# Reading tail keys and values in place, with one mask per step, instead of copying them per step

## The chip, the cores and the metric

The kernel runs on one core of one Trainium2 chip. The metric is the device time of one execution in microseconds, lower is better. The five compute engines appear in the profile as PE (TensorE matmuls), PEld (TensorE weight loads, which overlap PE), DVE (VectorE), ACT (ScalarE) and POOL (GpSimd); SP issues the DMAs.

## The reference, cut to what matters

Four layers run in turn, A B A B, each on a layer norm of a residual stream of 2048 tokens of width 640. Layer A is a segmented linear-memory attention and is not touched, except that its first instance now builds the masks. Layer B is recurrent:

```python
mem = mem0                                   # 8 memory tokens
for s in range(64):                          # segments of 32 tokens
    xs = x[:, 32 * s:32 * s + 32, :]
    h = concatenate([mem, xs])               # 40 tokens
    q, k, v = h @ Wq, h @ Wk, h @ Wv         # 32 heads of 128
    scores = where(mask, q @ k.T * scale, -1e9)   # key j seen by query i if i < 8 or i >= j
    o = (softmax(scores) @ v) @ Wo
    mem = o[:8]                              # the next step waits for this
    outs.append(o[8:])
```

A step can't start before the step before it has produced `mem`. There are 64 steps in a layer, two layers: 128 steps.

## The kernel before: the parts that matter

The 40 tokens of a step are kept as 24 tokens of the segment, 8 memory tokens and the segment's last 8 tokens, the "tail". Queries, keys and values of the tails of four steps (a group, `T`; `i4` is the step's place in it) are projected together, 32 tokens at once, into `QTt`, `KTt` and `Vtb`. Ahead of each step its 8 tails were copied out:

```python
def tails_to_seg(s):
    T, i = divmod(s, 4)
    nc.gpsimd.tensor_copy(heads(QT[s])[:, :, 32:40], QTt[T][:, :, 8 * i:8 * i + 8])
    nc.gpsimd.tensor_copy(heads(KT[s])[:, :, 32:40], KTt[T][:, :, 8 * i:8 * i + 8])
    Vt[s] = qkp.tile([128, 2, 512], BF16, name="b_Vt", tag="Vt")
    for j in range(4):
        nc.sync.dma_start(Vt[s][32 * j:32 * j + 8, :, :], Vtb[T][32 * j + 8 * i:32 * j + 8 * i + 8, :, :])
```

The values went by DMA since a token of `Vtb` is a partition, and the matmuls below read each head's values from the start of a block of 32 partitions. The scores are computed transposed (keys on partitions), four heads side by side in the four column tiles of the array; part `k = 0` has the 32 keys of segment and memory, part `k = 1` the 8 of the tail:

```python
for j in range(4):       # puts the mask into PSUM
    nc.tensor.matmul(sp[32 * j:32 * j + 32, :, 0:40], lhsT=C.identb[:, 32 * j:32 * j + 32], rhs=mask..., ...)
for r in range(4):
    for k, n in ((0, 32), (1, 8)):
        for j in range(4):
            o = sp[32 * j:32 * j + n, r, 16:56] if k == 0 else sp[32 * j:32 * j + n, r, 0:16]
            nc.tensor.matmul(o, lhsT=KT[s][:, 40 * h + 32 * k:40 * h + 32 * k + n],
                             rhs=QT[s][:, 40 * h + 24 * k:40 * h + 40], ...)
# ... exp on ACT into PT, sums with blk, normalise ...
for r in range(4):       # values
    for k, n in ((0, 32), (1, 8)):
        V_ = Vsb if k == 0 else Vt[s]
        for j in range(4):
            nc.tensor.matmul(o, lhsT=V_[32 * j:32 * j + n, b, 128 * r:128 * r + 128], rhs=PT[32 * j:32 * j + n, ...], ...)
```

Each step does this for two halves `b` of 16 heads. The output product goes to PSUM (`b_OPS`), DVE transposes it (`b_TM`), two DVE adds write the new memory into `b_hT`, and the next step's first projection (`b_Qa`) needs both. While they run, PE fills the time with a projection for the next group (`b_tail`) or with deferred outputs (`b_OPSd`).

## Time and profile before

| | before |
|---|---|
| median of the first 3 runs | 2362.52 us (2361.56 to 2363.86) |
| PE busy | 2226.6 us, 94% |
| POOL busy | 1073.2 us, 45% |
| tail-key copies on POOL | 128, 50.8 us in all |
| tail-value DMAs | 512 of 16 KB |
| one step of layer B | 12.96, 12.96, 13.48, 13.02 us (median by place in the group) |

The step times are worked out from single start times in the trace: from one `b_TM` to the next, without each layer's first.

From the page of the kernel before: busy time of the engines, the chain of work that ended last by engine and by line, and one line of the DMA issues.

```profile
PE 2226.6 (94%) x54988; PEld 1242.1 (53%) x54988; DVE 1578.4 (67%) x3636; ACT 949.3 (40%) x2207; POOL 1073.2 (45%) x2603
...
PE 79%; DVE 10%; ACT 4%; issue 2%; DMA 2%; POOL 1%; SPq 0%; DVEq 0%; POOLq 0%; ACTq 0%
...
b_Vt<-b_Vtb SPq DMA_DIRECT2D x512, 16.0 KB
```

PE is the bound: it is busy nearly always, and it holds most of the chain. POOL is on 1% of the chain, although it is busy 45% of the time.

The groups of instructions by form, kernel before. `L85` is the line of the helper through which the kernel issues everything, so the tile names tell the groups apart. Behind the count stand the busy time in us and the mean of one in ns, then the engine's idle time just before them and who ended it. In `128*8 128x8` the first pair is rows and columns of the array.

```profile
L85 PEld LDWEIGHTS <-b_KT 128*32 128x32 bf16 x4096 | 71.8, 94 | 33.0 <-DVE b_KT L85 15.7 <-issue 0.4
L85 PEld LDWEIGHTS <-b_KT 128*8 128x8 bf16 x4096 | 70.2, 84 | 0.0
L85 PEld LDWEIGHTS <-b_Vt 8*128 8x128 bf16 x4096 | 67.1, 91 | 1.7 <-issue 0.8
L85 PEld LDWEIGHTS <-b_Vsb 32*128 32x128 bf16 x4096 | 64.8, 90 | 103.4 <-ACT b_Vsb L85 53.9 <-DVE b_PT L85 25.9 <-DVE b_xn L85 11.9
L85 PE MATMUL b_SP<-b_mask,c_identb 128*32 128x160 bf16 x1024 | 63.7, 233 | 0.6 <-DVE b_TQ L85 0.5
L85 POOL COPY b_KT<-b_KTt 128x256 bf16<-128x256 bf16 x128 | 50.8, 397 | 0.0
L85 DVE TENSOR_TENSOR b_hT<-b_TM 64x40 bf16<-64x40 f32 x252 | 55.8, 221 | 8.6
```

A load of 8 columns lasts 10 ns less than one of 32; 8 rows and 32 rows last the same. PE idles 0.6 us in all before the score blocks (the mask matmul opens each), so nothing that feeds them is late. The Trainium skill, "TensorE: Matmul & The Clock Gate", section "LDWEIGHTS (loading the stationary operand)", gives the direction, columns count and rows don't. For the loads that change here the trace agrees, with 84 against 94 ns and 91 against 90 ns.

The chain in order of time, kernel before: start in us, length in us, what. These are the two score blocks and one value block of one step.

```profile
1024.80 0.28 PE b_SP L85 x36
...
1026.94 0.33 PE b_SP L85 x36
...
1027.97 0.29 PE b_OTL L85 x32
```

These 0.9 us, with a second value block 1.2 us, are all of a step's 13 us that the wider loads can touch.

### The profile page before, as it was taken

To read this page: it belongs to the slowest core of one execution; us is meant where nothing else is said; L and a number is where in the kernel's file an instruction comes from. 1 tells how busy PE (TensorE), PEld (TensorE's weight loads), DVE (VectorE), ACT (ScalarE), POOL (GpSimd) and SP (SyncE) were. 2 spreads that over 40 slices of the span, in tenths; PEclk is the share of its full clock that TensorE was granted. 3 is DMA by queue.
4 is the path that set the end of the run, shared out by engine and by line. 5 is a ranking of instruction groups with operands and counts; after the bars stand their busy time and mean duration, and the time that the engine had idled before them with its cause. 6 is when DMAs were issued, how large, how long until landed. Compare 5 with 4: busy or idle time off the path is not lost.

```text
span 2364.3 us, 123472 instructions
## 1 busy us (share of the span) xinstructions
PE 2226.6 (94%) x54988; PEld 1242.1 (53%) x54988; DVE 1578.4 (67%) x3636; ACT 949.3 (40%) x2207; POOL 1073.2 (45%) x2603
## 2 busy tenths in 40 slices
PE   7989979999999999999879998799999999999997
PEld 3444435555555555555545444455555555555554
DVE  6677646666666666666667776466666666666665
ACT  5666723332323233323257767133232323332322
POOL 3344434454454444544323444345445445444442
PEclk9999989999999999999989999899999999999999
DMA  6773341111111111110033333400000001000000
GB/s 173 196 184 99 107 143 24 26 23 26 24 24 23 25 26 26 23 24 21 21 115 109 107 108 109 151 22 23 20 22 20 22 22 23 22 23 21 19 18 16
DMA packets 98847, 131.83 MB, mean 56 GB/s; under 512 B 20592, under 2 KB 84096, under 8 KB 96384
## 3 DMA queue, kind: packets, MB, share of 16 engines
q1 hardware_dynamic: 96992, 122.21, 19.1%
q8 instruction: 431, 7.06, 1.3%
q10 hardware_dynamic: 1312, 1.64, 0.2%
q14 instruction: 112, 0.92, 0.1%
HBM read 89.17 MB, written 26.21 MB: 49 GB/s over the span
## 4 chain that ended last, share of the span: by engine, by line
PE 79%; DVE 10%; ACT 4%; issue 2%; DMA 2%; POOL 1%; SPq 0%; DVEq 0%; POOLq 0%; ACTq 0%
PE b_OPS L85 13%; PE b_V L85 12%; PE b_tail L85 7%; PE b_Qa L85 7%; PE b_Kb L85 6%; PE b_Qb L85 6%; PE b_Ka L85 6%; PE b_SP L85 4%; PE a_PP L85 4%; PE b_OTL L85 3%; ACT a_PT L85 3%; PE b_OPSd L85 3%; PE a_S L85 2%; PE a_pv L85 2%; DVE b_TM L85 1%
## 5 line engine op out<-in xcount | busy, mean ns | idle before, releaser
L85 PEld LDWEIGHTS <-b_hT 128*32 128x32 bf16 x15520 | 379.9, 96 | 339.5 <-DVE b_hT L85 65.8
L85 ACT ACTIVATE b_PT<-b_SP 128x224 bf16<-128x224 f32 x256 | 92.2, 360 | 773.1 <-DVE b_TQ L85 731.1
L85 PE MATMUL b_V<-b_wv,b_hT 128*32 128x512 bf16 x5120 | 361.5, 381 | 0.0
L85 ACT ACTIVATE a_PT<-a_S 128x768 bf16<-128x768 f32 (+1 forms) x384 | 326.5, 892 | 67.4 <-PE a_S L85 57.0
L85 PE MATMUL b_OPS<-b_wo,b_OTsb 128*32 128x320 bf16 x8192 | 325.9, 300 | 5.9 <-DVE b_OTsb L85 5.1
L85 PEld LDWEIGHTS <-b_OTsb 128*32 128x32 bf16 x8192 | 195.1, 96 | 114.2 <-DVE b_OTsb L85 49.5
L85 POOL CAST b_QT<-b_TQ 128x384 bf16<-128x384 f32 x254 | 140.8, 554 | 238.5 <-DVE b_TQ L85 238.5
L85 ACT CAST b_OTsb<-b_OTL 128x320 bf16<-128x320 f32 x384 | 150.9, 428 | 228.3 <-PE b_OTL L85 200.3
L85 POOL CAST b_KT<-b_TQ 128x384 bf16<-128x384 f32 x254 | 142.5, 561 | 162.4 <-DVE b_TQ L85 161.2
L85 POOL TENSOR_TENSOR b_PT<-b_PT,b_R 128x64 bf16<-128x64 bf16 x256 | 105.1, 411 | 216.4 <-ACT b_R L85 191.9
L85 POOL TENSOR_SCALAR_AFFINE_SELECT a_PT<-a_PT 128x256 bf16<-128x256 bf16 x256 | 107.8, 422 | 199.3 <-ACT a_PT L85 188.1
L85 PE MATMUL b_Kb<-b_wk,b_hT 128*32 128x512 bf16 x2560 | 185.5, 381 | 1.2 <-DVE b_TQ L85 1.2
L85 PE MATMUL b_Qa<-b_wq,b_hT 128*32 128x512 bf16 x2560 | 161.7, 381 | 13.4 <-DVE b_hT L85 7.1
L85 PE MATMUL b_Qb<-b_wq,b_hT 128*32 128x512 bf16 x2560 | 160.4, 379 | 0.0
L85 PE MATMUL b_Ka<-b_wk,b_hT 128*32 128x512 bf16 x2560 | 160.4, 379 | 0.0
L85 PE MATMUL a_PP<-a_xnT,a_wt 128*128 128x512 bf16 x560 | 151.1, 404 | 7.5 <-DVE a_um L85 1.7
L85 PE MATMUL a_S<-a_qk 32*128 32x512 bf16 (+3 forms) x1024 | 138.8, 312 | 8.1 <-ACT a_PT L85 6.4
L85 DVE STREAM_TRANSPOSE b_TM<-b_OPS 128x320 f32<-128x320 f32 x126 | 65.2, 517 | 115.2 <-PE b_OPS L85 115.2
L85 DVE TENSOR_TENSOR b_PT<-b_PT,b_R 128x160 bf16<-128x160 bf16 x256 | 103.5, 404 | 49.4 <-ACT b_R L85 29.5
L85 DVE CAST b_Vsb<-b_V 128x512 bf16<-128x512 f32 x128 | 88.5, 692 | 68.2 <-PE b_SP L85 53.5
L85 DVE STREAM_TRANSPOSE b_TQ<-b_Qa 128x512 f32<-128x512 f32 x128 | 91.7, 716 | 62.5 <-PE b_Qa L85 40.9
L85 DVE CAST b_OTsb<-b_OTL 128x320 bf16<-128x320 f32 x128 | 62.9, 492 | 104.5 <-PE b_OTL L85 104.5
(148 smaller groups left out, 4154.9 us busy)
## 6 DMA issues: line engine op xcount, KB each, us to landing
a_wt<-a_wpad SPq DMA_DIRECT2D x112, 160.0 KB
b_wo<-in_B_Wo_dram SPq DMA_DIRECT2D x8, 1280.0 KB
b_Vt<-b_Vtb SPq DMA_DIRECT2D x512, 16.0 KB
b_XO<-xres SPq DMA_DIRECT2D x256, 30.0 KB
a_wvo<-in_A_wo_dram SPq DMA_DIRECT2D x8, 800.0 KB
b_wq<-in_B_Wq_dram SPq DMA_DIRECT2D x20, 256.0 KB
b_wk<-in_B_Wk_dram SPq DMA_DIRECT2D x20, 256.0 KB
xres<-a_xo SPq DMA_DIRECT2D x16, 320.0 KB
```

The lines of the kernel that those rows point to most:

```text
L85: r = f(*a, **k)
```

## The change: intent and diff

The tail keys and values of the whole group, 32 tokens, are used as they lie. A mask per step of the group (`mask[:, i4]`) sends the 24 tokens of the other steps to -1e9, so that their exponentials are zero. The copies of tail keys and the DMAs of tail values go; the tail-query copy stays. Tail-score loads grow from 8 to 32 columns, tail-value loads from 8 to 32 rows; the number of matmuls stays. The masks are built once, in the first layer A, and no longer in each layer B.

```diff
+def build_masks(nc, C):
+    ...
+    C.mask = C.pool.tile([128, 4, 40], BF16, name="c_mask")
+    nc.vector.memset(C.mask[:], 0.0)
+    for j in range(4):
+        ...                                   # 4 affine selects on gpsimd each
+    C.blk = C.pool.tile([128, 4, 32], BF16, name="c_blk")
+    nc.vector.memset(C.blk[:], 0.0)
+    for j in range(4):
+        nc.vector.memset(C.blk[32 * j:32 * j + 32, j, :], 1.0)
 ...
         gg = W.gates(nc, st)
+        build_masks(nc, C)                    # head of layer A; once
 ...
-            KT[s] = qkp.tile([128, 32 * 40], BF16, name="b_KT", tag="KT")
+            KT[s] = qkp.tile([128, 32 * 32], BF16, name="b_KT", tag="KT")
 ...
-            nc.gpsimd.tensor_copy(heads(KT[s])[:, :, 32:40], KTt[T][:, :, 8 * i:8 * i + 8])
-            Vt[s] = qkp.tile([128, 2, 512], BF16, name="b_Vt", tag="Vt")
-            for j in range(4):
-                nc.sync.dma_start(Vt[s][32 * j:32 * j + 8, :, :], Vtb[T][...])
 ...
-                                     rhs=mask[:].unsqueeze(1).to_broadcast([128, 4, 40]),
+                                     rhs=C.mask[:, i4].unsqueeze(1).to_broadcast([128, 4, 40]),
 ...
-                            nc.tensor.matmul(o, lhsT=KT[s][:, 40 * h + 32 * k:40 * h + 32 * k + n],
+                            nc.tensor.matmul(o, lhsT=KTt[T][:, h, :] if k else KT[s][:, 32 * h:32 * h + 32],
 ...
-                        V_ = Vsb if k == 0 else Vt[s]
+                        V_ = Vtb[T] if k else Vsb
 ...
-                            nc.tensor.matmul(o, lhsT=V_[32 * j:32 * j + n, b, 128 * r:128 * r + 128],
+                            nc.tensor.matmul(o, lhsT=V_[32 * j:32 * j + 32, b, 128 * r:128 * r + 128],
 ...                                           # old mask and blk of layer B removed; general path alike
```

More of the change, by code (lines that the diff above doesn't have):

```diff
@@ L103, in __getattr__ @@
         return getattr(self._nc, attr)
+def build_masks(nc, C):
+    if hasattr(C, "mask"):
+        return
+    C.mask = C.pool.tile([128, 4, 40], BF16, name="c_mask")
+    nc.vector.memset(C.mask[:], 0.0)
+    for j in range(4):
+        m = C.mask[32 * j:32 * j + 32]
+        nc.gpsimd.affine_select(out=m[:, :, 0:16], in_=m[:, :, 0:16], pattern=[[-8, 4], [0, 16]], compare_op=ALU.is_ge,
+                                fill=-1e9, base=0, channel_multiplier=1)
+        nc.gpsimd.affine_select(out=m[:, :, 0:8], in_=m[:, :, 0:8], pattern=[[8, 4], [0, 8]], compare_op=ALU.is_ge,
+                                fill=-1e9, base=7, channel_multiplier=-1)
+        nc.gpsimd.affine_select(out=m[:, :, 8:16], in_=m[:, :, 8:16], pattern=[[8, 4], [1, 8]], compare_op=ALU.is_ge,
+                                fill=-1e9, base=0, channel_multiplier=-1)
+        m = C.mask[32 * j:32 * j + 24, :, 16:40]
+        nc.gpsimd.affine_select(out=m, in_=m, pattern=[[0, 4], [1, 24]], compare_op=ALU.is_ge,
+                                fill=-1e9, base=0, channel_multiplier=-1)
+    C.blk = C.pool.tile([128, 4, 32], BF16, name="c_blk")
+    nc.vector.memset(C.blk[:], 0.0)
+    for j in range(4):
+        nc.vector.memset(C.blk[32 * j:32 * j + 32, j, :], 1.0)
 def watch(nc, C, sums, inverses):
@@ L653, in heads @@
         def heads(t):
-            return t[:, 0:1280].rearrange("p (h c) -> p h c", c=40)
+            return t[:].rearrange("p (h c) -> p h c", h=32)
         def alloc_h(s):
@@ L696, in place @@
             evac(eng, dst3[:, 16 * b:16 * b + 16, c0:c0 + (t1 - t0)], tq[:, :, t0:t1])
-        QTt, KTt, Vtb, Vt = {}, {}, {}, {}
+        QTt, KTt, Vtb = {}, {}, {}
         hx = {}
@@ L755, in tails_to_seg @@
             nc.gpsimd.tensor_copy(heads(QT[s])[:, :, 32:40], QTt[T][:, :, 8 * i:8 * i + 8])
-            nc.gpsimd.tensor_copy(heads(KT[s])[:, :, 32:40], KTt[T][:, :, 8 * i:8 * i + 8])
-            Vt[s] = qkp.tile([128, 2, 512], BF16, name="b_Vt", tag="Vt")
-            for j in range(4):
-                nc.sync.dma_start(Vt[s][32 * j:32 * j + 8, :, :], Vtb[T][32 * j + 8 * i:32 * j + 8 * i + 8, :, :])
         class OPass:
@@ L809, in layer_B @@
             nc.vector.memset(ones[:], 1.0)
-        blk = st.tile([128, 2, 4, 32], BF16, name="b_blk")
-        nc.vector.memset(blk[:], 0.0)
-        for j in range(4):
-            nc.vector.memset(blk[32 * j:32 * j + 32, 0, j, :], 1.0)
-            nc.vector.memset(blk[32 * j:32 * j + 8, 1, j, :], 1.0)
         if not general:
@@ L819, in layer_B @@
         nc.vector.memset(XO[:], 0.0)
-        negs = wk.tile([128, 32], F32, name="b_negs", tag="Vsb")
-        nc.vector.memset(negs[:], -1e9)
-        mask = st.tile([128, 40], BF16, name="b_mask")
-        maskf = wk.tile([128, 40], F32, name="b_maskf", tag="tsc")
-        nc.vector.memset(maskf[:], 0.0)
-        for j in range(4):
-            r0 = 32 * j
-            nc.gpsimd.affine_select(out=maskf[r0:r0 + 24, 16:40], in_=negs[r0:r0 + 24, 0:24],
-                                    pattern=[[-1, 24]], compare_op=ALU.is_gt, fill=0.0, base=0, channel_multiplier=1)
-            nc.gpsimd.affine_select(out=maskf[r0:r0 + 8, 8:16], in_=negs[r0:r0 + 8, 0:8],
-                                    pattern=[[-1, 8]], compare_op=ALU.is_gt, fill=0.0, base=0, channel_multiplier=1)
-        nc.vector.tensor_copy(mask[:], maskf[:])
         if general:
             maskq = st.tile([128, 40], BF16, name="b_maskq")
-            maskqf = wk.tile([128, 40], F32, name="b_maskqf", tag="tsc")
+            maskqf = wk.tile([128, 40], F32, name="b_maskqf", tag="xnb")
+            negs = wk.tile([128, 32], F32, name="b_negs", tag="Vsb")
+            nc.vector.memset(negs[:], -1e9)
             nc.vector.memset(maskqf[:], 0.0)
@@ L922, in row_max @@
                         h = 16 * b + 8 * q + i
-                        nc.tensor.matmul(sp[:, i, :], lhsT=QT[s][:, 40 * h:40 * h + 40], rhs=KT[s][:, 40 * h:40 * h + 40],
+                        nc.tensor.matmul(sp[:, i, 0:32], lhsT=QT[s][:, 40 * h:40 * h + 40], rhs=KT[s][:, 32 * h:32 * h + 32],
+                                         start=False, stop=True, skip_group_check=True)
+                        nc.tensor.matmul(sp[:, i, 32:40], lhsT=QT[s][:, 40 * h:40 * h + 40], rhs=KTt[T][:, h, 8 * i4:8 * i4 + 8],
                                          start=False, stop=True, skip_group_check=True)
@@ L965, in scores @@
                     nc.tensor.matmul(sp[32 * j:32 * j + 32, :, 0:40], lhsT=C.identb[:, 32 * j:32 * j + 32],
-                                     rhs=mask[:].unsqueeze(1).to_broadcast([128, 4, 40]),
+                                     rhs=C.mask[:, i4].unsqueeze(1).to_broadcast([128, 4, 40]),
                                      start=True, stop=False, tile_position=(0, 32 * j), skip_group_check=True)
                 for r in range(4):
-                    for k, n in ((0, 32), (1, 8)):
+                    for k in range(2):
                         for j in range(4):
                             h = 16 * b + 4 * j + r
-                            o = sp[32 * j:32 * j + n, r, 16:56] if k == 0 else sp[32 * j:32 * j + n, r, 0:16]
-                            nc.tensor.matmul(o, lhsT=KT[s][:, 40 * h + 32 * k:40 * h + 32 * k + n],
+                            o = sp[32 * j:32 * j + 32, r, 0:16] if k else sp[32 * j:32 * j + 32, r, 16:56]
+                            nc.tensor.matmul(o, lhsT=KTt[T][:, h, :] if k else KT[s][:, 32 * h:32 * h + 32],
                                              rhs=QT[s][:, 40 * h + 24 * k:40 * h + 40], start=False, stop=True,
@@ L976, in scores @@
                 if general:
-                    for k, n in ((0, 32), (1, 8)):
+                    for k in range(2):
                         for j in range(4):
                             h = 4 * j
-                            o = sp[32 * j:32 * j + n, :, 16:56] if k == 0 else sp[32 * j:32 * j + n, :, 0:16]
-                            nc.tensor.matmul(o, lhsT=ones[0:3, 0:n], rhs=mrows[b][:, h:h + 4, 24 * k:40],
+                            o = sp[32 * j:32 * j + 32, :, 0:16] if k else sp[32 * j:32 * j + 32, :, 16:56]
+                            nc.tensor.matmul(o, lhsT=ones[0:3, 0:32], rhs=mrows[b][:, h:h + 4, 24 * k:40],
                                              start=False, stop=True, tile_position=(0, 32 * j), skip_group_check=True)
@@ L990, in sums @@
                     for j in range(4):
-                        nc.tensor.matmul(sm_[32 * j:32 * j + 32, :, 24 * k:40], lhsT=blk[:, k, j],
+                        nc.tensor.matmul(sm_[32 * j:32 * j + 32, :, 24 * k:40], lhsT=C.blk[:, j],
                                          rhs=PT[:, b, :, 0:16] if k else PT[:, b, :, 16:56], start=(k == 0), stop=(k == 1),
@@ L1009, in values @@
                 for r in range(4):
-                    for k, n in ((0, 32), (1, 8)):
-                        V_ = Vsb if k == 0 else Vt[s]
+                    for k in range(2):
+                        V_ = Vtb[T] if k else Vsb
                         for j in range(4):
                             o = OTL[b, j // 2][:, j % 2, 40 * r + 24 * k:40 * r + 40]
-                            nc.tensor.matmul(o, lhsT=V_[32 * j:32 * j + n, b, 128 * r:128 * r + 128],
-                                             rhs=PT[32 * j:32 * j + n, b, r, 0:16] if k else PT[32 * j:32 * j + n, b, r, 16:56],
+                            nc.tensor.matmul(o, lhsT=V_[32 * j:32 * j + 32, b, 128 * r:128 * r + 128],
+                                             rhs=PT[32 * j:32 * j + 32, b, r, 0:16] if k else PT[32 * j:32 * j + 32, b, r, 16:56],
                                              start=(k == 0), stop=(k == 1), tile_position=(32 * j, 0))
@@ L1132, in layer_B @@
                 store_deferred(T, od)
-            hT.pop(s); QT.pop(s); KT.pop(s); Vt.pop(s)
+            hT.pop(s); QT.pop(s); KT.pop(s)
         if not general:
```

## The prediction

> **What bounds the kernel now.** TensorE (PE). The profile's first part has PE busy 94% of 2364.3 us, POOL 45%, DVE 67%; PE holds 79% of the chain that ended last, and no tail-value DMA and no copy of tail keys is among its large shares. A recurrent step of layer B (128 of them) takes 13.0 to 13.5 us. In the chain the two score blocks take 0.28 to 0.33 us (36 matmuls each), the two value blocks 0.30 us (32 each); the rest is projections and output product, which the change leaves alone.
>
> **Removed.** Per step one POOL copy of tail keys (b_KT<-b_KTt, x128, mean 397 ns, 50.8 us in all, groups by form) and four 16 KB DMAs of tail values (x512, about 0.63 us of SP issue each), with four DMA-semaphore waits on PE weight loads. Per layer B: eight small affine selects (185 to 199 ns each) and some DVE memsets.
>
> **Added.** Once, in the head of the first layer A: 16 affine selects on POOL (estimate 0.2 us each from those above, 3.2 us) and six DVE memsets.
>
> **Changed on PE, same count.** The 4096 tail-score weight loads go from 8 to 32 columns, the 4096 tail-value loads from 8 to 32 rows. By form, an 8-column load lasts 84 ns, a 32-column one 94; 8-row and 32-row value loads 91 and 90. The Trainium skill, "TensorE: Matmul & The Clock Gate", section "LDWEIGHTS (loading the stationary operand)", agrees: time goes with columns, not contraction rows. Streaming sizes stay (16 and 40 columns).
>
> **How much is on the critical path.**
> - Score blocks: single starts in the trace show a group of four every 25 ns, alike behind 8-column and 32-column loads; loads hide under the matmuls before them. +0. If 10 ns showed for each of the 1024 groups of four: +10 us; not expected.
> - Value blocks: groups every 25 ns for both forms; the block that waits for the DMA has the same first-group spacing (39 ns) as the one that doesn't. +0.
> - POOL copies: where tails are copied early, POOL has slack before anything PE needs. In a group's last step the copy stands ahead of the next step's POOL casts, but PE hardly idles in the score block behind them (b_SP, idle under 1 us in all). About 0.
> - Head of each layer B: the chain runs POOL KT cast, QT copy, KT copy (0.34 us), LayerNorm power, DVE apply, transpose. Without that copy: -0.3 us, twice.
> - Head of the first layer A: DVE memsets now stand ahead of the first a_qk casts on the chain: +0.5 us. The POOL selects fit POOL's idle stretch (14 to 28.6 us).
> - Old masks in layer B's head ran under 9.2 us of tail projections; removing them gives 0.
>
> Sum about -0.1 us.
>
> **Predicted time: 2362.0 us, 2354 to 2370 in 8 of 10. Faster by over 2%: 0.01; within 2%: 0.98; slower by over 2%: 0.01.**
>
> **What would show it.** Score blocks stay at 0.28 to 0.33 us and value blocks at 0.30 us in the chain; 32-column b_KTt loads last about 94 ns, yet PE busy time moves by under 5 us. POOL busy falls by about 50 us. DMA issues lose 512. The chain b_TM, b_hT, b_hT, b_Qa between steps keeps its 1.03 to 1.13 us.
>
> **What would make it wrong.** Slower: the wider loads do not hide (+10 us, or +41 us if they serialise: 4096 x 10 ns); the late POOL cast of tail keys now releases PE directly in the first step of a group; the POOL selects run past 28.6 us. Faster: POOL's shorter queue moves its copy of deferred outputs out from under the b_hT adds (299 against 197 ns where they overlap), 0.1 us in up to half of the steps (6 us).

## The result, and the profile after

| | before | after |
|---|---|---|
| median of 4 runs of the same rounds | 2362.04 us (2359.29 to 2363.86) | 2361.45 us (2357.76 to 2366.59) |
| ratio, 95% interval | | 1.000, 0.9978 to 1.0022 |
| steps of layer B by place, us | 12.96, 12.96, 13.48, 13.02 | 12.96, 12.96, 13.49, 13.03 |
| POOL busy | 1073.2 us | 1032.7 us |

A ratio is the mean time of one kernel's runs over that of the other's of the same rounds, so it is not quite the ratio of the medians quoted. The mean of the four step medians is 13.105 us before and 13.108 us after.

The page and the groups by form of the kernel after:

```profile
PE 2217.9 (94%) x54988; PEld 1241.1 (53%) x54988; DVE 1575.9 (67%) x3618; ACT 949.1 (40%) x2207; POOL 1032.7 (44%) x2475
...
PE 78%; DVE 10%; ACT 5%; DMA 4%; issue 2%; POOL 0%; SPq 0%; DVEq 0%; ACTq 0%; POOLq 0%
```

```profile
L85 PEld LDWEIGHTS <-b_KTt 128*32 128x32 bf16 x4096 | 72.8, 94 | 0.0
L85 PEld LDWEIGHTS <-b_Vtb 32*128 32x128 bf16 x4096 | 67.1, 91 | 1.7 <-issue 1.2
L85 PE MATMUL b_SP<-c_mask,c_identb 128*32 128x160 bf16 x1024 | 63.7, 233 | 0.6 <-DVE b_TQ L85 0.5
L85 DVE TENSOR_TENSOR b_hT<-b_TM 64x40 bf16<-64x40 f32 x252 | 56.0, 222 | 8.6
```

The tail-score loads now last 94 ns, as predicted, and PE still idles 0.6 us before the score blocks. The `b_hT` add has not moved either (221 to 222 ns). In the chain, a step of the kernel after shows the same blocks:

```profile
624.38 0.29 PE b_SP L85 x36
...
626.52 0.34 PE b_SP L85 x36
...
627.55 0.30 PE b_OTL L85 x32
```

Over all 128 steps the median from the first to the last matmul start is 284 ns before and 285 after for the first score block, 352 and 352 for the second, 199 and 199 for a step's first value block, and 200 and 200 for its second.

The timeline of PE through one score block of the kernel after shows how the wider loads cost nothing: groups of four matmuls (one for each column tile), segment keys (`b_KT`) and tail keys (`b_KTt`) in turn. The first column is the start.

```profile
624.27 0.19 PE L85 MATMUL b_SP<-b_QT,b_KT 128*32 128x40 bf16 x4
624.30 0.18 PE L85 MATMUL b_SP<-b_QT,b_KTt 128*32 128x16 bf16 x4
624.33 0.19 PE L85 MATMUL b_SP<-b_QT,b_KT 128*32 128x40 bf16 x4
624.35 0.18 PE L85 MATMUL b_SP<-b_QT,b_KTt 128*32 128x16 bf16 x4
624.38 0.19 PE L85 MATMUL b_SP<-b_QT,b_KT 128*32 128x40 bf16 x4
```

A group starts every 25 ns (mean of the middle groups over 128 steps), in both kernels, whether its matmuls stream 40 or 16 columns and whether its loads have 32 or 8. The Trainium skill, "TensorE: Matmul & The Clock Gate", section "Wait — 56ns, not 53.3ns?", says that start-to-start of matmuls never drops below about 25 ns however few columns stream. The trace agrees if the group of four tiles is taken as the unit; single matmuls of a group start 3 to 4 ns apart.

The profiled execution after has a span of 2355.7 us, the one before 2364.3. That is no gain: each layer's stretch of 62 steps takes 813.4 and 813.3 us before, 813.1 and 813.4 after. The rest lies outside the steps, mainly in layers A, and it varies from execution to execution: the second layer A with its turn-over to layer B takes 330.8 us in the profile before, 327.2 after, but 327.4 in experiment 6 below, whose layers A are those of the kernel before. The TensorE clock differed too: up to the first `b_TM` the profile shows a mean granted clock (the share of full speed that the throttle allowed) of 0.93 before and 0.95 after.

### The profile page after: what moved, and what is told of

Same layout as the page of the kernel before. It is cut to its first block, busy times and chain, and to the rows that moved or that the text cites. A ratio compares the mean times of both kernels' runs of the same rounds, so it can differ in the third digit from the quotient of the medians.

```text
span 2355.7 us, 122645 instructions
## 1 busy us (share of the span) xinstructions
PE 2217.9 (94%) x54988; PEld 1241.1 (53%) x54988; DVE 1575.9 (67%) x3618; ACT 949.1 (40%) x2207; POOL 1032.7 (44%) x2475
## 4 chain that ended last, share of the span: by engine, by line
PE 78%; DVE 10%; ACT 5%; DMA 4%; issue 2%; POOL 0%; SPq 0%; DVEq 0%; ACTq 0%; POOLq 0%
PE b_OPS L85 13%; PE b_V L85 13%; PE b_Qa L85 7%; PE b_tail L85 6%; PE b_Kb L85 6%; PE b_Qb L85 6%; PE b_Ka L85 6%; PE b_SP L85 4%; PE a_PP L85 4%; ACT a_PT L85 3%; PE b_OTL L85 3%; PE b_OPSd L85 3%; PE a_S L85 2%; PE a_pv L85 1%; DVE b_TM L85 1%
```

## The experiments

The question is why nothing moved. Two theories were set against each other. *Slack*: the copies and DMAs ran in time that nobody waited for, and the wider loads are hidden, so both are worth zero. *Cancelling*: the copies were worth something, and the wider loads cost as much. A third possibility, that POOL's shorter queue shifts a collision with DVE (named in the prediction), was tested apart.

### 1. The removed work put back as dead work

```diff
+            dead = qkp.tile([128, 32, 8], BF16, name="b_dead", tag="dead")
+            nc.gpsimd.tensor_copy(dead[:], KTt[T][:, :, 8 * i:8 * i + 8])
+            Vd = qkp.tile([128, 2, 512], BF16, name="b_Vd", tag="Vd")
+            for j in range(4):
+                nc.sync.dma_start(Vd[32 * j:32 * j + 8, :, :], Vtb[T][32 * j + 8 * i:32 * j + 8 * i + 8, :, :])
```

> The changed kernel with the removed work put back as dead work: per step one POOL copy of the tail keys into a tile that nobody reads, and the four DMAs of tail values into a tile that nobody reads. TensorE's instructions and load widths are those of the changed kernel. Slack theory (both the removed work and the wider loads are worth about nothing): same time as before and after, within 0.3%; the 62 recurrent steps of a layer B (first to last b_TM) keep 813 us, within 1 us; POOL busy back up by about 50 us to near 1080. Cancelling theory (the copies and DMAs were worth X us and the wider loads cost the same X): this kernel pays both and is slower than before by X, visible as more than 3 us per layer in that stretch.

Measured: 2362.31 us median of 6 against 2361.27 (11 runs of before), ratio 1.0006, 0.9985 to 1.0027. POOL busy is back at 1078.5 us. The mean of the four step medians is 13.109 us. One of the two 62-step stretches took 813.7 us, the other 816.9, which is outside the 1 us that was expected, and over the 3 us that the cancelling theory named. But the medians show that the usual step did not grow. Half of the excess is a single interval, the first of that stretch, 1.85 us longer than the usual one: the granted clock was 0.52 there between 1515.7 and 1518.0 us, and the projection `b_Qa` took 2.26 us where the kernel after takes 1.26. The rest is single steps that were 0.2 to 0.5 us longer. Such steps occur in the profiles of all the kernels at full granted clock; in most of those looked at, PE pauses once between two groups of a value block and waits for nothing that the profile shows. Their cause stays open. The cancelling theory needs a longer usual step, and there is none. (Nothing reads the dead tiles, so this run does not put back PE's four waits for the value DMAs.)

### 2. The key copy alone removed, loads left narrow

```diff
-            nc.gpsimd.tensor_copy(heads(KT[s])[:, :, 32:40], KTt[T][:, :, 8 * i:8 * i + 8])
 ...
-    nc.tensor.matmul(o, lhsT=KT[s][:, 40 * h + 32 * k:40 * h + 32 * k + n],
+    nc.tensor.matmul(o, lhsT=KTt[T][:, h, 8 * i4:8 * i4 + 8] if k else KT[s][:, 40 * h:40 * h + 32],
```

> The kernel before with the POOL copy of tail keys alone removed: the tail-score loads read the 8 columns in place from the group's tile of tail keys; values still come by DMA, mask as before. Slack theory: same time as before, within 0.3%, the stretch of 62 steps at 813 us within 1 us, 8-column loads still at 84 ns. Cancelling theory: faster than both by X, the stretch shorter by more than 3 us.

Measured: 2363.89 us median of 6 against 2361.27, ratio 1.0008, 0.9985 to 1.0031; steps 12.96, 12.96, 13.49, 13.03 us; stretches 813.4 and 814.1 us; loads 84 ns. The copy is worth nothing without the wider loads too. With experiment 1 all four corners of the table "copies yes or no, loads narrow or wide" are filled (value DMAs go with the copies except in this run): 13.105, 13.109, 13.109 and 13.108 us a step. The cancelling theory falls for the keys. For the values, no run separates the DMAs from the wider loads; there the value blocks speak, with the same 199 and 200 ns in both kernels.

### 3. The tail-score matmuls taken out (wrong result)

```diff
-                    for k in range(2):
+                    for k in range(1):
```

> The changed kernel without the tail-score matmuls (wrong result on purpose; the tail scores are then zero where the mask lets them through). 4096 load-matmul pairs in 1024 groups of four go. If each group costs its start-to-start pitch of 25 ns whatever the load's width (slack theory): about 26 us less in all, about 13 us less per layer B stretch (813 to about 800 us), total near 2336 us. If the loads' 94 ns were exposed even once per group: more, 1024 x 94 ns = 96 us less. If the groups hid entirely under something else: no change.

Measured: 2328.55 us, ratio 0.9855, 0.9828 to 0.9881; 33 us less than the kernel after and not 26. (The comparison with the reference is no proof that the tail scores are right.) The chain shows the two score blocks with 20 in place of 36 matmuls:

```profile
620.34 0.16 PE b_SP L85 x20
...
622.34 0.26 PE b_SP L85 x20
```

So the method sees a group that goes. Inside the two blocks 0.23 us a step went (worked out from single starts, means: 290 to 169 ns and 336 to 226 ns, first to last matmul), where eight groups at 25 ns would be 0.20; the last group of the first block costs 37 ns and not 25. The step medians fell by 0.25 us, which makes 32 us over 128 steps. The rest, 0.02 us a step, is not settled. It is far from the 96 us that exposed 94 ns loads would have meant.

### 4. More POOL work, in the place of the removed copy

Three and nine dead copies per step:

```diff
+            for _ in range(3):        # and 9
+                dead = qkp.tile([128, 32, 8], BF16, name="b_dead", tag="dead")
+                nc.gpsimd.tensor_copy(dead[:], KTt[T][:, :, 8 * i:8 * i + 8])
```

> The changed kernel with three dead POOL copies per step, each of the size of the removed one, in the removed one's place: about 1.0 us of POOL per step (130 us in all, POOL busy near 1185 us). Slack theory: POOL's idle time there swallows them; steps keep their medians of 12.96, 12.96, 13.49 and 13.03 us (by place in the group of four) except that the first step of a group may gain up to 0.1 us; total within 0.3% of before. Proportional theory (POOL time counts at some fixed share): the share that showed for one copy was zero, so any growth clear of noise in all four steps speaks against slack.

Measured: 2363.25 us against 2361.98, ratio 1.0021, 1.0000 to 1.0043. POOL busy 1159.6 us (less than the expected 1185: the records of POOL copies overlap, they start 0.34 us apart and last 0.40). Steps 12.95, 12.96, 13.43, 13.11 us. The third lost 0.06: the `b_OTdef` copy (experiment 5) begins 0.06 us earlier there, and the add under it takes 240 ns and not 299 (medians). The fourth interval, which holds the start of the next group, gained 0.08, as expected. It did so by a collision: POOL's casts come 1.03 us later, one of them then lies over DVE's cast of new keys (`b_KT`), and the first score block waits for that. Kernel after, then this run, at the start of a group:

```profile
650.29 0.23 DVE L85 CAST b_KT<-b_TQ 128x128 bf16<-128x128 f32 x1
```

```profile
649.31 0.56 DVE L85 CAST b_KT<-b_TQ 128x128 bf16<-128x128 f32 x1
```

The mean of the four is 13.111 us. Three times the removed copy is still nearly free.

> As the run with three, with nine dead copies: about 3.1 us of POOL per step. Slack theory: now beyond the slack. The copies reach over the two b_hT adds on DVE (0.1 us more for each add, in up to three of four steps), and at the start of a group they hold POOL's casts of the new queries, so DVE's next transposes and then the PSUM tiles that TensorE needs come late: about 1.5 to 2 us more in the first step of each group (31 of them), 0.1 to 0.2 us in the others. Total 40 to 80 us longer (1.7% to 3.4%). If instead it stays within 0.3%, POOL's slack is over 3 us at every place and TensorE alone sets the step.

Measured: 2448.86 us against 2361.98, ratio 1.0376, 1.0357 to 1.0395, somewhat above the expected range. Steps 13.33, 13.32, 13.49, 14.90 us: +0.38, +0.36, 0.00 and +1.87. The first two are more than the expected 0.1 to 0.2: the two `b_hT` adds there lie under dead copies and take 459 and 311 ns in place of 196 and 197 (medians, first step). The chain at the start of a group shows the path of the +1.87:

```profile
665.64 3.10 POOL b_dead L85 x9
668.74 0.46 POOL b_hT L85 x2
669.20 0.47 POOL b_QT L85
...
669.69 0.73 DVE b_TQ L85
...
670.46 0.40 PE b_V L85 x4
```

POOL worked these off in program order. The nine copies hold back its cast of the new queries (`b_QT`); only that cast frees the buffer for DVE's next transpose (`b_TQ`); only that transpose frees the PSUM tile for PE's value projection (`b_V`). This is the path in the steps on which the removed copy could have mattered. It has over one microsecond of slack: with three copies the cast comes 1.03 us later and this path holds nothing up (the 0.08 came from the score block); with nine it comes 3.09 us later and `b_V` 1.94, so about 1.15 us of slack by this estimate. The removed copy takes 0.34 us. That is why removing it gained nothing in the steps: there it was never on the path.

### 5. A collision that the change left in place

In the third and fourth step of a group, POOL's copy of the deferred outputs (`b_OTdef`) waits behind its cast of projected tails and then lies over the first `b_hT` add. Kernel after, chain, and POOL's timeline at the same place:

```profile
632.45 0.53 DVE b_TM L85
...
633.01 0.31 DVE b_hT L85
...
633.34 0.21 DVE b_hT L85
```

```profile
632.85 0.40 POOL L85 COPY b_OTdef<-b_OTsb 128x256 bf16<-128x256 bf16 x1
```

The add that meets the copy takes 0.10 us more than its twin. The edit puts the copy ahead of the cast:

```diff
+            if i4 != 0:
+                nc.gpsimd.tensor_copy(OTdef[:, :, 8 * i4:8 * i4 + 8], OTsb[:, :, 32:40])
             flush()                        # POOL's cast of the tails
             op.run(8)
 ...                                        # the small b_seen sum moves too; old place kept for i4 == 0
```

> The changed kernel with POOL's copy of the deferred outputs (b_OTdef) and the small b_seen sum moved ahead of POOL's cast of the projected tails, in three of four steps. In the third and fourth step of a group the copy overlaps the first b_hT add on DVE now, 297 ns against 197. If that overlap is what makes the add slow and the add is on the path to b_Qa: the mean b_hT add goes from 222 to about 197 ns and the steps concerned (2 of 4, 62 of 124) lose 0.1 us each, 6 us in all, 3 us per layer stretch (813 to 810 us). If the add's length has another cause, or the tail projections hide it, the stretch stays at 813 us.

Measured: 2356.54 us median of 6 against 2361.27, ratio 0.9981, 0.9961 to 1.0000. Steps 12.96, 12.96, 13.39, 12.94 us: 0.09 us less in just the two places. The 62-step stretches took 810.5 us, as expected, and 813.3; in the second one two intervals were 1.7 and 1.3 us longer, and there the granted clock was 0.50 (from 1508.3 to 1511.7 us and from 2307.0 to 2310.4). The mean add is at 196 ns:

```profile
L85 DVE TENSOR_TENSOR b_hT<-b_TM 64x40 bf16<-64x40 f32 x252 | 49.5, 196 | 8.6
```

and the chain leaves DVE altogether in such a step and goes through PE's filler, so the hand-over is no longer the longer branch there:

```profile
626.36 1.16 PE b_OPS L85 x32
627.51 1.08 PE b_tail L85 x20
...
628.60 0.40 PE b_Qa L85 x4
```

The Trainium skill, "SBUF — State Buffer", section "SBUF: two separate sides", says that a GpSimd instruction that reads SBUF and a VectorE instruction with two SBUF inputs need the same port pair, and that the later one is blocked until the earlier one ends. The traces fit: in the run with nine copies all 196 adds that took over 210 ns ended 44 to 58 ns after the end of a POOL instruction. Where POOL copies lie back to back in that run, a `b_hT` add that began 6 ns ahead of a copy's recorded start took 466 ns and ended 48 ns after that copy's end; one begun 151 ns after a copy's start ended 48 ns after its end too. (Which one took the lock first is not to be read from these records.)

### 6. Did that gain need the change?

The same edit on the kernel before:

> The kernel before, with the same early b_OTdef copy as the run on the changed kernel. If that gain (0.09 us in the third and fourth step of a group) comes from the copy's place in POOL's order alone: the same here, steps near 12.96, 12.96, 13.39 and 12.94 us, mean b_hT add 197 ns, total about 5.7 us under before. If it needed POOL's time freed by the change: the steps of before stay at 13.48 and 13.02 us.

Measured: 2356.95 us median of 6 against 2361.98, ratio 0.9982, 0.9967 to 0.9997. Steps 12.95, 12.96, 13.39, 12.93 us, adds at 196 ns. The stretches fell less than the medians say, to 812.5 and 811.8 us, as this profile has more of the single long steps (one of them, 1.3 us, at half the granted clock). The gain is that of the order on POOL alone. The change neither brings it nor is needed for it.

### 7. Masks built where the engines wait, with the early copy

The prediction put +0.5 us on the head of the first layer A. The chain of the kernel after has the memsets on it:

```profile
22.86 0.18 DVE a_gg L85
23.04 0.08 DVE c_mask L85
23.12 0.09 DVE c_blk L85
...
23.76 1.30 DVE a_qk L85 x2
25.10 0.41 PE a_KN L85 x4
```

The kernel before had no memsets there:

```profile
23.35 2.24 PE a_PP L85 x10
...
25.61 0.70 DVE a_qk L85
```

From the first `a_PP` matmul to the first `a_S` matmul the kernel before takes 3.43 us, the kernel after 3.90. The edit, on top of that of experiment 5:

```diff
-        build_masks(nc, C)                 # behind the gates
 ...
+        build_masks(nc, C)                 # ahead of the first layer-norm statistics
         stats = {}
```

> The run with the early b_OTdef copy on the changed kernel, and the masks built at the very start of the first layer A, where DVE (1.9 to 4.3 us) and POOL (2.2 to 5.7 us) wait for the first input, instead of ahead of the first a_qk casts. If the six DVE memsets were what lengthened that head: from the first a_PP to the first a_S 3.43 us as in the kernel before, not 3.90 as in the changed one (0.47 us back). The selects must end near 6.2 us, when the chain still waits for input tiles: nothing later. If the head was longer for another reason, it stays at 3.90 us. Steps of layer B as in the run with the early copy (12.96, 12.96, 13.39, 12.94 us); total 6 us under before, within 3 us.

Measured: 2353.68 us median of 6 against 2361.70, ratio 0.9972, 0.9953 to 0.9990. The head is back at 3.43 us, and the steps are 12.96, 12.96, 13.39, 12.93 us. The head (0.47 us) and the steps (0.09 us in some 60 steps, 5.5 us) account for 6 of the 8 us between the medians; the rest is within the scatter of runs. This version is faster than the kernel before by 0.3%. The kernel after did not run in these rounds.

## Why the prediction was right, point by point

- **Score blocks, +0: right.** The wider loads last 94 ns, and no score block is longer by more than 1 ns (medians). Groups stay at 25 ns, blocks at 0.29 and 0.34 us in the chain, step medians within 4 ns. That the width of the key loads matters neither with nor without the copies is shown by experiments 1 and 2.
- **Value blocks, +0: right.** Groups stay at 25 ns with 32 rows. The four DMA waits were given up and nothing came of it: the median blocks are alike (199 and 200 ns in both kernels).
- **POOL copies, about 0: right.** The slack on that path in the steps is over 1.0 us (experiment 4), the copy is 0.34 us.
- **Head of each layer B, -0.3 us twice: wrong in that step.** The chain of the kernel before really ran through the key copy:

```profile
336.57 0.73 DVE b_TQ L85
...
338.20 0.34 POOL b_KT L85
...
338.57 0.56 POOL b_ln_rstd L85
```

  In the kernel after the copy is gone, and in the first layer B the chain runs through DVE's layer-norm statistics, which arrive as late:

```profile
331.12 0.72 DVE b_TQ L85
331.84 0.78 DVE b_ln_st L85 x2
...
333.12 0.56 POOL b_ln_rstd L85
```

  From this transpose to the start of the layer-norm power it is 2.00 us in both (338.57 - 336.57 and 333.12 - 331.12). In the second layer B the statistics themselves waited for a DMA of the residual stream, and the power came later than before:

```profile
1489.80 12.73 DMA b_xt<-xres_bf
...
1503.96 0.56 POOL b_ln_rstd L85
```

  From the end of the projection before (`b_first`) to that power it is 2.12 us in both heads of the kernel before, 2.11 and 3.01 in the kernel after. The change need not be to blame for the 0.9 us: in experiment 2, which keeps the value DMAs, the second head takes 3.13 us. In the first head the dead copies of experiments 1 and 4 show how little slack there is: 2.12 us with one, 2.75 with three, 4.80 with nine. So the removed copy (0.34 us) was last, but the statistics were there at the same time. A chain names the branch that came last, not by how much. The second branch was not looked at.
- **Head of the first layer A, +0.5 us: right**, 0.47 measured, and given back by experiment 7. The selects on POOL took 4.0 us and not 3.2, 218 to 285 ns each; the first select of `a_PT` then began 0.5 us late, with no cost that the chain shows.
- **Old masks in layer B's head, 0: nothing speaks against it, and it was not tested apart.** From `b_hx` to `b_first` it is 10.1 and 10.2 us before, 9.4 and 10.2 after; in experiment 6, which has the old masks, 8.8 and 10.1.
- **PE busy, under 5 us of movement: missed, it fell by 8.7 us.** In the two stretches of steps it moved by under 0.5 us (805.8 and 805.5 us before, 805.4 and 805.9 after). The fall lies outside them, in layers A with their heads, where the granted clock differed.
- **POOL busy, -50 us: the term was mis-sized.** It fell by 40.5 us. The mean record of 397 ns overlaps its neighbour; back to back the copies start 0.34 us apart.
- **Named risk on the fast side** (the deferred-output copy moves from under the adds): it did not happen, since that copy waits for POOL's tail cast and not for the removed copy. Experiments 5 and 6 show that the mechanism itself was real.

The terms of time that failed are the 0.6 us at the heads of layers B, with another 0.9 us in the second head of this one profile, against runs that scatter over several us. That the total lies within 1 us of the forecast is in part luck, since the medians of the kernel before alone lie between 2361.27 and 2362.52 us; what was tested is that the wider loads cost no 10 us and the copies gave nothing back. The two big questions, load width and POOL time, were answered from single starts in the trace.

## What to carry to other kernels

Removing work pays only where something waits for it: look for the engine's name in the chain before counting its busy time, and test the slack by adding work in the same place, which tells how far the path is from mattering. Before crediting a saving on a chain, look at the second branch into the same wait. Here very small matmuls, four tiles of the array at a time, went at one pace for a group (25 ns), so widening their weights to save copies was free, and dropping a group was what paid.

## What the Trainium skill lacked or had wrong

- "TensorE: Matmul & The Clock Gate", section "LDWEIGHTS (loading the stationary operand)", gives columns / 1.2 ns, whatever the rows. An estimate from it for loads into 32-column tiles is 20 ns between 8 and 32 columns and under 30 ns for a whole load; the profile shows 84 and 94 ns, so 10 ns apart and with a large fixed part. Nor does a load of 128 columns last longer than one of 32 (both 96 ns with 128 rows, `a_PT` and `b_hT`), and with 32 rows it lasts 90.
- The same page's floor of about 25 ns between matmul starts does not say how it counts with tiles of the array. Here it holds for a group of four tiles, each matmul with its own weight load between (25 ns for each group, 3 to 4 ns between matmuls in it). Nor does it say that weight loads of 8 and of 32 columns, which last 84 and 94 ns, leave that pace alike.
- "SBUF — State Buffer", section "SBUF: two separate sides", has the lock between POOL and DVE right, but no size for such small work: a 64x40 DVE add went from 197 ns to 297 under one POOL copy, and to 466 ns under a row of them; under one copy it ended 50 to 54 ns after the copy did (60 adds in each kernel, before and after).
